# The Fourier step numbered by remainders to 64 and 47, with the first batch's blocks turned by TensorE

## The chip, the cores and the metric

The kernel runs on one core of one Trainium2 chip. A core has five engines with a queue of instructions each: TensorE (PE, with weight loads shown apart as PEld), VectorE (DVE), ScalarE (ACT), GpSimd (POOL) and SyncE (SP), which here only issues DMAs. An engine takes its instructions in the order of its queue; an instruction that waits for another engine holds up all that stands behind it.

The metric is the device time of one execution, as the median of several runs: 2486.35 us for the kernel before.

## What is computed

```python
X = np.fft.rfft(x, axis=1)                       # x: 8 batches, 3008 tokens, 256 columns
y = np.fft.irfft(X * (filt_r + 1j * filt_i), n=3008, axis=1)
h = y.reshape(24064, 256) @ w_in                 # 256 x 2048
g = h * (1.0 / (1.0 + np.exp(-1.702 * h)))
out = g @ w_out                                  # 2048 x 256
```

A real Fourier transform over 3008 tokens, a product with a filter, the transform back, and a two-layer network on every token. The weights come as 64-bit floats.

## The kernel before

**The transform.** 3008 = 64 x 47. Token 47 n1 + n2 stands at (n1, n2). The first step is, for each n2, a product with a 64 x 64 matrix over n1; in this numbering the matrix differs for every n2, since it holds the twiddle factors too. Pairs of n2 share the 128 rows: `t1` has 24 matrices, `t2` the 24 for the way back. The result is laid out by s (32 places), and the second step is, for each s, a product with a 47 x 47 matrix `d` over n2 (called s2 here). Then comes the product with the filter, then `e` (called i2), and last `t2` (i1). Between first and second step the data have to change places between partitions and columns. That goes through DRAM: `a_d` on the way in, `b_d` on the way back.

**Batch 0** is done by `first_fft` (from L301) before all else, in plain float32, in two halves of 128 columns. `load_t1` (L273) loads the first tables and spreads them with copies; `first_step` (L353) makes the first products (L360) and writes them to `a_d`; `load` reads them back into `z_zy` and `z_wi`; sixteen times follow s2 (L409), `product` (L429: three DVE instructions from PSUM, L433 to L435, and a sum on POOL, L436), i2 (L414), a copy on ACT (L415) and a store to `b_d` (L418). `load_f` loads a filter piece to partitions 0 to 47 and copies it to 64 to 111 on ACT (L333).

**Batches 1 to 7** are done by `fft` (L445) in pieces beside the network of the batch ahead, each operand split in a high and a low part in the float32r format (`mm3`, L257). L456 to L463 are its first step, `forward` and `backward` the others, with the same `product`, here from SBUF.

**The network.** 48 tiles of up to 512 tokens: `signal` (L552) makes i1 of the tile (L559) from `br` and splits it into `y`; `mlp` (L573) runs 16 chunks of h (L588, six products), the activation on ACT (L592, L593), the low part gl on DVE (L594) and six products into o (L602).

**The weights** are loaded and turned from 64-bit to two float32r parts by `weights` (L228) in 16 pieces, on ACT (L208, L218, L224), DVE (L213 to L219) and POOL (L217, L225). The first pieces are begun after `first_fft`, the others in the first tile's 16 chunks.

**What sets the order.** A scheduler orders each engine's queue by its own estimate of times; instructions given to `keep_in_program_order` stay as written. PSUM banks for batch 0 come in turn from three pools (`bank`, L265). SP's loads stay in program order until the middle of the first tile.

Of the kernel before, what the change touches and what calls it, by code (L numbers as in the profile page):

```python
# [17 lines left out]
N1, N2 = 64, 47  # L18
# [11 lines left out]
def _tables():  # L30
# [22 lines left out]
    t1 = np.zeros((P, NH, N1))  # L53
    t2 = np.zeros((P, NH, P))
    for j in range(2):
        for q in range(NH):
            n2 = NH + q if j else NH - 1 - q
            if n2 >= N2:
                continue
            for s in range(NS):  # L60
                if s == 0:
                    re, im = np.ones(N1), np.where(n1 % 2, -1.0, 1.0) * (-1.0 if j else 1.0)
                    ire, iim = re / S, im / S
                else:
# [34 lines left out]
    return t1.astype(np.float32), t2.astype(np.float32), de.astype(np.float32)  # L99


def _places():


    n1, q = np.arange(N1), np.arange(NH)
    n2 = np.stack([NH - 1 - q, NH + q])
    time = np.where(n2[:, None, :] < N2, N2 * n1[None, :, None] + n2[:, None, :], S)
    p, s = np.arange(48)[:, None], np.arange(NS)[None, :]
    high = np.where(s == 0, 32 + 64 * (p - 24), 64 - s + 64 * (p - 24))
    freq = np.where(p < 24, s + 64 * p, np.where((p < 47) | (s == 0), high, S // 2 + 1))  # L110
# [11 lines left out]
    return time, freq, np.concatenate(token)  # L122


def _layout(a):

    x, fr, fi, wi, wo = a
    time, freq, _ = _places()
    x = np.concatenate([x, np.zeros((B, 1, D), x.dtype)], 1)[:, time]
    x_0 = x[0].reshape(P, 3, 8, 2, P).transpose(3, 1, 0, 2, 4)  # L130
    x_r = x[1:].reshape(B - 1, P, 6, 4, D).transpose(0, 2, 1, 3, 4)
    f = np.stack([fr, fi], 1)
    f = np.concatenate([f, np.zeros((1, 2, D), f.dtype)])[freq]
# [7 lines left out]
def tile_kernel(  # L141
    ctx: ExitStack,
    tc: tile.TileContext,
    x_0: bass.AP,
    x: bass.AP,
    filt_0: bass.AP,
# [32 lines left out]
    t1_sb = const.tile([P, NH, 2, P], F32R, name="t1_sb")  # L179
    t2_sb = const.tile([P, NH, P], F32, name="t2_sb")  # L180
    de_sb = const.tile([Q, 2, 4, Q], F32R, name="de_sb")
    HALF = NFC // 2
    wi_sb, wo_sb = [], []
# [87 lines left out]
    t1_f, de_of = [], []  # L271

    def load_t1(q):  # L273
        hs = slice(12 * q, 12 * q + 12)
        st = sb.tile([P, 12, 2, 32], F32, tag="out", name=f"t1_{q}")
        load_in(st, t1[:, hs].rearrange("p h (k s) -> p h k s", k=2))
        tf = sb.tile([P, 12, 2, 2, 32], F32, tag="y", name=f"t1f_{q}")
        t1_f.append(tf.rearrange("p h j k s -> p h (j k s)"))
        nc.scalar.copy(tf[:, :, 0], st)
        for k in range(2):  # L280
            nc.vector.tensor_copy(tf[0:64, :, 1, k], st[0:64, :, 1 - k])
            nc.vector.tensor_scalar(tf[64:128, :, 1, k], st[64:128, :, 1 - k], -1.0, None, ALU.mult)

    def split_t1(q):
        hs = slice(12 * q, 12 * q + 12)
        nc.scalar.copy(t1_sb[:, hs, 0], t1_f[q])
        nc.vector.tensor_tensor(t1_sb[:, hs, 1], t1_f[q], t1_sb[:, hs, 0].bitcast(F32), ALU.subtract)

    def split_de(de_f):
# [3 lines left out]
        pin = tc.keep_in_program_order  # L293
        pin(nc.gpsimd.memset(de_sb.bitcast(F32), 0.0))
# [6 lines left out]
    def first_fft():  # L301
# [25 lines left out]
        def load_f(g, load_in=load_in):  # L327
# [4 lines left out]
            for i in range(0, n, 8):  # L332
# [3 lines left out]
                if i:  # L336
                    tc.keep_in_program_order(ins)
# [372 lines left out]
```

## Time and profile before

| what | value |
|---|---|
| device time, three runs | 2485.58, 2486.35, 2490.07 us |
| the profiled execution's own time | 2489.39 us |
| its span, first to last instruction | 2487.6 us |
| mean granted clock of TensorE | 0.987 |
| DMA traffic | 254.76 MB, 102 GB/s over the span |

The page of the profile gives busy time by engine; the groups of instructions give one row for each line, engine, operation and tile, with the mean of one; the waits say which engine stood idle until what. An engine's busy time says nothing of which stage it falls in, and a mean over the span mixes the opening with the long part behind it. The lines that matter stand in the prediction.

### The profile page before, as it was taken

How to read it: one execution, taken by the hardware profiler on the slowest of the kernel's cores; microseconds unless marked ns; L12 is line 12 of the kernel's file. 1: busy time of each engine (PE TensorE's matmuls, PEld its weight loads, DVE VectorE, ACT ScalarE, POOL GpSimd, SP SyncE). 2: the span in 40 equal slices, each digit the busy share in tenths (PEclk: the TensorE clock that was granted, in tenths of full speed). 3: DMA queues.
4: the chain of work that ended last, by engine and by line, in shares of the span. 5: the costliest groups of instructions: out<-in, count | busy, mean ns of one | idle time of the engine just before them, and what ended most of it. 6: DMA issues, size and time to landing. Idle time of an engine off the chain costs nothing.

```text
span 2487.6 us, 31904 instructions
## 1 busy us (share of the span) xinstructions
PE 2397.4 (96%) x11132; PEld 1986.7 (80%) x11132; DVE 1550.9 (62%) x2169; ACT 1315.1 (53%) x2399; POOL 825.9 (33%) x716
## 2 busy tenths in 40 slices
PE   5689999999999999999999999999999999999999
PEld 3368778878887888988888888888888888898887
DVE  6784895498636874478835787367753788432322
ACT  4555565555555555555555555555555555444443
POOL 3472553255324432254313443234421344100000
PEclk8789999999999999999999999999999999999999
DMA  8745443554345433544345343544434443300000
GB/s 202 213 123 148 103 114 103 150 109 113 98 136 118 107 85 90 153 99 106 75 135 126 94 96 83 148 113 104 101 92 129 101 105 83 73 15 9 18 9 18
DMA packets 154145, 254.76 MB, mean 102 GB/s; under 512 B 16112, under 2 KB 94048, under 8 KB 153696
## 3 DMA queue, kind: packets, MB, share of 16 engines
q1 hardware_dynamic: 71776, 137.46, 20.4%
q10 hardware_dynamic: 57056, 70.80, 10.8%
q0 software_dynamic: 25152, 44.45, 9.0%
q8 instruction: 89, 1.46, 0.2%
q14 instruction: 72, 0.59, 0.1%
HBM read 155.65 MB, written 96.99 MB: 102 GB/s over the span
## 4 chain that ended last, share of the span: by engine, by line
PE 75%; DMA 4%; DVE 2%; ACT 1%; issue 1%; SPq 0%; POOL 0%; ACTq 0%; POOLq 0%; DVEq 0%
PE o L602 33%; PE h L588 33%; PE i L559 3%; DMA br<-b_d 2%; PE s L494 2%; PE i L494 2%; DMA b_d<-b 1%; PE s L259 1%; PE s L260 1%; PE s L258 1%; DMA zy<-a_d 1%; DVE gl L594 1%; DMA a_d<-al 1%; DMA x<-in_x_dram 1%; SPq L174 0%
## 5 line engine op out<-in xcount | busy, mean ns | idle before, releaser
L588 PE MATMUL h<-y,wi 128*128 128x512 f32 (+1 forms) x4608 | 1174.6, 388 | 8.1 <-ACT wi L224 4.9
L594 DVE TENSOR_TENSOR gl<-g,gh 128x512 fp32r<-128x512 f32 (+1 forms) x768 | 648.3, 847 | 757.2 <-ACT gh L593 710.6
L588 PEld LDWEIGHTS h<-y,wi 128*128 128x128 f32 x4608 | 863.9, 189 | 178.9 <-ACT wi L224 5.4
L592 ACT ACTIVATE g<-h 128x512 f32<-128x512 f32 (+1 forms) x768 | 452.6, 590 | 926.3 <-PE h L588 820.8
L602 PE MATMUL o<-gh,wo 128*128 128x512 f32 (+1 forms) x3072 | 834.0, 390 | 8.4 <-ACT gh L593 6.4
L602 PEld LDWEIGHTS o<-gh,wo 128*128 128x128 f32 x3072 | 567.0, 189 | 122.7 <-ACT gh L593 11.1
L602 PE MATMUL o<-gl,wo 128*128 128x512 f32 (+1 forms) x1536 | 479.7, 388 | 9.4 <-DVE gl L594 9.3
L593 ACT ACTIVATE gh<-h 128x512 fp32r<-128x512 f32 (+1 forms) x768 | 449.0, 585 | 46.9 <-PE o L602 43.2
L509 POOL TENSOR_TENSOR zy<-c_buf,zy 48x512 fp32r<-48x512 f32 x224 | 330.9, 1477 | 92.1 <-DVE zy L508 82.0
L602 PEld LDWEIGHTS o<-gl,wo 128*128 128x128 f32 x1536 | 285.2, 189 | 67.1 <-DVE gl L594 13.6
L436 POOL TENSOR_TENSOR c_buf<-c_buf,u_buf 112x512 f32<-112x512 f32 x128 | 183.3, 1432 | 465.7 <-DVE c_buf L435 464.6
L456 POOL TENSOR_TENSOR xl<-x,xh 128x512 fp32r<-128x512 f32 x84 | 112.6, 1352 | 416.1 <-ACT xh L455 357.5
L477 POOL DMA_DIRECT2D zy<-a_d x224 | 128.1, 574 | 293.6 <-DMA a_d<-ah 80.1
L443 DVE TENSOR_TENSOR c_buf<-s,c_buf 48x512 f32<-48x512 f32 x224 | 154.1, 688 | 22.5 <-ACT c_buf L442 16.4
L443 DVE TENSOR_TENSOR b<-i,b 48x512 f32<-48x512 f32 x224 | 154.0, 687 | 8.4 <-ACT b L442 2.0
L442 ACT COPY c_buf<-s 48x512 f32<-48x512 f32 x224 | 130.2, 581 | 19.9 <-PE s L494 9.8
L442 ACT COPY b<-i 48x512 f32<-48x512 f32 x224 | 130.1, 581 | 14.5 <-PE i L494 4.1
L559 PEld LDWEIGHTS i<-t_sb,br 128*128 128x128 f32 x736 | 101.5, 196 | 36.4 <-DVE w_tu L215 8.2
L508 DVE CAST zy<-c_buf 48x512 fp32r<-48x512 f32 x224 | 100.0, 447 | 44.4 <-POOL c_buf L436 40.5
L559 PE MATMUL i<-t_sb,br 128*128 128x128 f32 x736 | 106.4, 282 | 21.9 <-DMA br<-b_d 20.9
L570 POOL CAST y<-carry 128x128 fp32r<-128x128 f32 x8 | 3.2, 429 | 266.0 <-PE h L588 265.9
L434 DVE TENSOR_TENSOR u_buf<-c_buf,f_buf 48x512 f32<-48x512 f32 x112 | 87.1, 778 | 3.6
(91 smaller groups left out, 1343.9 us busy)
## 6 DMA issues: line engine op xcount, KB each, us to landing
f_buf<-in_filt_dram SPq DMA_DIRECT2D x224, 192.0 KB, 3.3
zy<-a_d POOLq DMA_DIRECT2D x224, 192.0 KB, 3.6
x<-in_x_dram SPq DMA_DIRECT2D x48, 512.0 KB, 4.9
b_d<-b ACTq DMA_DIRECT2D x128, 192.0 KB, 2.6
out_dram<-out SPq DMA_DIRECT2D x44, 512.0 KB, 3.7
a_d<-ah ACTq DMA_DIRECT2D x84, 256.0 KB, 3.5
a_d<-al ACTq DMA_DIRECT2D x84, 256.0 KB, 3.8
br<-b_d SPq DMA_DIRECT2D x84, 256.0 KB, 4.7
```

The costliest lines, as they stand in the source:

```text
L436: nc.gpsimd.tensor_tensor(u1, u1, u2, ALU.add)
L442: nc.scalar.copy(dst[h], ps[k][o])
L443: nc.vector.tensor_tensor(dst[h], ps[k][h], dst[h], ALU.add)
L456: nc.gpsimd.tensor_tensor(xl, src, xh.bitcast(F32), ALU.subtract)
L477: nc.gpsimd.dma_start(zy[0][64 * k : 64 * k + 48, i % 2].rearrange("p k s d -> p k (s d)"), src.rearrange("n k s d -> n k (s d)"),)
L509: nc.gpsimd.tensor_tensor(y[o, k], u1[h], y[h, k].bitcast(F32), ALU.subtract)
L559: nc.tensor.matmul(ps[:, P * i : P * i + P], br[m][:, i], t2_sb[:, 4 * t + i, :], start=True, stop=True)
L588: nc.tensor.matmul(ps[:, :w], wi_sb[half][:, wk, kc, c], y[:, yk, kc, :w], start=n == 0, stop=n == 5)
L592: nc.scalar.activation(g[:, :w], ps[:, :w], AF.Gelu_apprx_sigmoid)
L593: nc.scalar.activation(gh[:, :w], ps[:, :w], AF.Gelu_apprx_sigmoid)
L594: nc.vector.tensor_tensor(gl[:, :w], g[:, :w], gh[:, :w].bitcast(F32), ALU.subtract)
L602: nc.tensor.matmul(pos[m][:, :w], wo[:, wk, P * m : P * m + P], gp[gk][:, :w], start=fc == 0 and n == 0, stop=fc == NFC - 1 and n == 2,)
```

## The change

**Numbering.** Place (n1, n2) now holds token (47 n1 + 64 n2) mod 3008, and a frequency is numbered by its remainders to 64 and to 47. In this numbering the two steps separate: the first matrix is the same for all n2, so `t1` and `t2` are one 128 x 128 matrix each. In exchange some of the needed frequencies stand where their mirror image is computed, so the imaginary part of the product needs a sign by place: `sign`, one column per s. `product` takes two s with different signs at a time, and reads the sign per partition: four DVE instructions of 256 columns in place of two of 512.

**Tables.** All tables come in one DRAM tensor `tabs` and lie in one SBUF tile `tab`; the first 128 columns are loaded by a DMA of their own.

**Batch 0 stays on chip.** The first step takes x as the stationary operand, so its result has columns of x on the partitions; ACT and DVE copy it to `a_t` ordered by s. For each pair of s TensorE transposes four blocks of `a_t` into PSUM, ACT copies them to `zs`, and s2 follows. i2 takes the product as the stationary operand, in four products of 96 columns, and ACT copies the result to `b_t`. `signal` transposes blocks of `b_t` into PSUM, and ACT or DVE copies them to `br`. `a_d` and `b_d` of batch 0, and the ACT copies of the filter, are gone; each filter piece is now loaded by two DMAs.

**Batches 1 to 7** keep their way through DRAM. `mm3` in the first step now covers two n2 in one go of 512 columns.

```diff
-                for i in range(2):
-                    h = 4 * c + 2 * u + i
-                    mm3(ps[:, i, :], t1_sb[:, h, 0, :], t1_sb[:, h, 1, :], xh[:, i, :], xl[:, i, :])
+                mm3(ps, t1_sb[:, 0], t1_sb[:, 1], xh, xl)
...
-        nc.vector.scalar_tensor_tensor(u2[0:48], xs[64:Q], -1.0, f_i[64:Q], ALU.mult, ALU.mult)
-        nc.vector.tensor_tensor(u2[64:Q], xs[0:48], f_i[0:48], ALU.mult)
+        for u in range(2):
+            for h, o in ((slice(0, 48), slice(64, Q)), (slice(64, Q), slice(0, 48))):
+                sg = sign[h, 2 * i + u : 2 * i + u + 1]
+                nc.vector.scalar_tensor_tensor(u2[o, u], xs[h, u], sg, f_i[h, u], ALU.mult, ALU.mult)
         nc.vector.tensor_tensor(u1, xs[:Q], f_r, ALU.mult)
         nc.gpsimd.tensor_tensor(u1, u1, u2, ALU.add)
...
+        w = WIDTHS["t1_0"]
+        pin(nc.scalar.dma_start(tab[:, 0:w], tabs[:, 0:w]))
+        xrs = [raw(f"x_0_{c}") for c in range(6)]
+        for c in range(6):
+            load_in(xrs[c], x[0, c])
+            if c == 3:
+                pin(nc.scalar.dma_start(tab[:, w:], tabs[:, w:]))
...
+        for c in range(6):
+            for m in range(2):
+                ps = bank(f"s1_0_{c}_{m}").rearrange("p a d -> p (a d)").rearrange("p (i c) -> p i c", i=4)
+                for i in range(4):
+                    nc.tensor.matmul(ps[:, i], xrs[c][:, i, P * m : P * m + P], table["t1_0"], start=True, stop=True)
+                src = ps.rearrange("p i (a s) -> p s a i", s=NS)
+                dst = a_t[m].rearrange("p s (a q) -> p s a q", q=NH)[:, :, :, 4 * c : 4 * c + 4]
+                (nc.vector.tensor_copy if m else nc.scalar.copy)(dst, src)
+        yield
+        for g in range(16):
+            if 6 <= g + 6 < 16:
+                load_f(g + 6)
+            z_ps = bank(f"z_0_{g}")
             for u in range(2):
+                for m in range(2):
+                    nc.tensor.transpose(z_ps[:96, u, P * m : P * m + P], a_t[m][:, 2 * g + u], table["eye"])
+            z = sb.tile([96, 2, D], F32, tag="half", name=f"zs_0_{g}", bufs=4)
+            nc.scalar.copy(z, z_ps[:96])
+            ps = bank(f"s2_0_{g}")
+            ms = [(slice(0, 1), 1), (slice(1, 2), 0)] if g == 0 else [(slice(0, 2), 0)]
+            for u, m in ms:
+                nc.tensor.matmul(ps[:Q, u], d_0[:96, m], z[:, u], start=True, stop=True)
+            u1 = c_buf[g % 3]
+            product(g, ps, u1, f_s[g % 8])
+            ps = bank(f"i2_0_{g}").rearrange("p a d -> p (a d)")[:, 0:384].rearrange("p (m u c) -> p m u c", m=2, u=2)
+            for u in range(2):
+                for m in range(2):
+                    nc.tensor.matmul(ps[:, m, u], u1[:Q, u, P * m : P * m + P], e_0[:Q, int(g + u == 0)], start=True, stop=True)
+            nc.scalar.copy(b_t[:, :, :, 2 * g : 2 * g + 2], ps.rearrange("p m u c -> p m c u"))
             yield
...
+            if b == 0:
+                ps = ps_f.tile([P, 4, P], F32, tag="f", name=f"bt_{t}_{m}")
+                for i in range(4):
+                    q = 4 * (4 * t + i)
+                    nc.tensor.transpose(ps[:, i], b_t[:, m, q : q + 4].rearrange("p c s -> p (c s)"), table["eye"])
+                br = {m: sb.tile([P, 4, P], F32, tag="half", name=f"br_{b}_{t}_{m}", bufs=4)}
+                (nc.vector.tensor_copy if m else nc.scalar.copy)(br[m], ps)
...
-        if i in (4, 5, 6):
+        if i in (2, 5, 8, 11):
             run(w_parts, 1)
-        if i == 5:
-            br = next(first_b)
-    next(first_b)
-    run(w_parts, 5)
-    run(start(0, 0, br))
+    run(w_parts, 4)
+    run(start(0, 0))
```

TensorE's queue in `first_fft`, from the first i2 on, before. The name `s_0_5` is s2 of group 5, `i_0_1` is i2 of group 1 (L409 and L414):

```order
L409 MATMUL s_0_2_264<-z_zy,de_f 112x512
L409 MATMUL s_0_3_273<-z_zy,de_f 112x512
L409 MATMUL s_0_4_287<-z_zy,de_f 112x512
L414 MATMUL i_0_0_246<-c_buf_78,de_f 112x128
L414 MATMUL i_0_0_246<-c_buf_78,de_f 112x384
L409 MATMUL s_0_5_296<-z_zy,de_f 112x512
L414 MATMUL i_0_1_256<-c_buf_79,de_f 112x512
L409 MATMUL s_0_6_315<-z_zy,de_f 112x512
L414 MATMUL i_0_2_270<-c_buf_80,de_f 112x512
```

The same place now; `z_2` names the four transpositions (L342) of group 2, copied to `zs_2` on ACT before s2 of group 2 can read it:

```order
L348 MATMUL s_0_0_208<-zs_0_206,tab 112x256 x2
L354 MATMUL i_0_0_217<-tab,c_buf_78 128x96 x4
L348 MATMUL s_0_1_232<-zs_1_230,tab 112x512
L342 MATMUL z_2_250<-tab,a_t_85 96x128
L342 MATMUL z_2_250<-tab,a_t_86 96x128
L342 MATMUL z_2_250<-tab,a_t_85 96x128
L342 MATMUL z_2_250<-tab,a_t_86 96x128
L348 MATMUL s_0_2_257<-zs_2_255,tab 112x512
L354 MATMUL i_0_1_240<-tab,c_buf_79 128x96 x4
```

Before, s2 of groups 0 to 4 stood ahead of i2 of group 0, and s2 stayed five ahead. Now s2 of group 1 stands behind i2 of group 0, and s2 of group 2 ahead of i2 of group 1. The queue goes on in the same way in turn, to the end of the sixteen groups:

```order
L354 MATMUL i_0_2_265<-tab,c_buf_80 128x96 x4
L348 MATMUL s_0_3_280<-zs_3_278,tab 112x512
L342 MATMUL z_4_296<-tab,a_t_85 96x128
L342 MATMUL z_4_296<-tab,a_t_86 96x128
L342 MATMUL z_4_296<-tab,a_t_85 96x128
L342 MATMUL z_4_296<-tab,a_t_86 96x128
L348 MATMUL s_0_4_303<-zs_4_301,tab 112x512
L354 MATMUL i_0_3_288<-tab,c_buf_78 128x96 x4
```

So the s2 of every odd group moved behind the i2 of the even group ahead of it.

DVE's queue in the middle of the program, where batch 3's transform runs beside the network: one group before (`c_buf` holds s2's result, `gl_1_10` is the low part of chunk 10 of a tile):

```order
L443 TENSOR_TENSOR c_buf_78<-s_3_6_1_7323,c_buf_78 48x512
L434 TENSOR_TENSOR u_buf_81<-c_buf_78,f_buf 48x512
L433 SCALAR_TENSOR_TENSOR u_buf_81<-c_buf_78,f_buf 48x512
L594 TENSOR_TENSOR gl_1_10_6752<-g_1_10_6750,gh_1_10_6751 128x512
L435 TENSOR_TENSOR c_buf_78<-c_buf_78,f_buf 112x512
```

and the same group now:

```order
L374 TENSOR_TENSOR c_buf_78<-s_3_6_1_7467,c_buf_78 48x512
L365 SCALAR_TENSOR_TENSOR u_buf_81<-c_buf_78,tab,f_buf 48x256 x4
L521 TENSOR_TENSOR gl_1_12_6953<-g_1_12_6951,gh_1_12_6952 128x512
L366 TENSOR_TENSOR c_buf_78<-c_buf_78,f_buf 112x512
```

Four instructions of half the width stand ahead of gl where two stood.

More of the change, by code (lines that the diff above doesn't have):

```diff
@@ L149, in tile_kernel @@
     w_out: bass.AP,
-    t1: bass.AP,
-    t2: bass.AP,
-    de: bass.AP,
+    tabs: bass.AP,
     out: bass.AP,
@@ L176, in load_in @@
             tc.keep_in_program_order(ins)
-    t1_sb = const.tile([P, NH, 2, P], F32R, name="t1_sb")
-    t2_sb = const.tile([P, NH, P], F32, name="t2_sb")
+    tab = const.tile([P, sum(WIDTHS.values())], F32, name="tab")
+    t1_sb = const.tile([P, 2, P], F32R, name="t1_sb")
     de_sb = const.tile([Q, 2, 4, Q], F32R, name="de_sb")
     HALF = NFC // 2
+    table, at = {}, 0
+    for name, w in WIDTHS.items():
+        table[name] = tab[:, at : at + w]
+        at += w
+    t2_sb, sign = table["t2"], table["sign"]
     wi_sb, wo_sb = [], []
@@ L269, in bank, with split_de @@
         return pool.tile([P, 2, D], F32, tag=tag, name=name)
[L271 to L289, printed above, removed]
+    def split_de():
         pin = tc.keep_in_program_order
+        de_f = table["de"].rearrange("p (m c) -> p m c", m=4)
+        pin(nc.scalar.copy(t1_sb[:, 0], table["t1"]))
+        pin(nc.vector.tensor_tensor(t1_sb[:, 1], table["t1"], t1_sb[:, 0].bitcast(F32), ALU.subtract))
         pin(nc.gpsimd.memset(de_sb.bitcast(F32), 0.0))
@@ L314, in first_fft @@
-        f_in = [f_0, f_1[0], f_1[1], f_2[0], f_2[1], f_1[0], f_1[1], f_0]
-        f_loads = {0: (1, f_0), 1: (2, f_1[2]), 3: (1, f_2[0]), 4: (1, f_2[1]), 5: (2, f_1[2]), 7: (1, f_0)}
-        def clean(eng, *ts):
-            for t in ts:
-                tc.keep_in_program_order(eng.memset(t[32:64], 0.0))
-        clean(nc.vector, f_0)
-        clean(nc.gpsimd, *c_buf)
-        a_d = [dram1.tile([48, 64, H], F32, name=f"a_d0_{i}") for i in range(2)]
-        b_d = b_of[0] = [dram1.tile([48, 64, H], F32, name=f"b_d0_{i}") for i in range(2)]
@@ new lines, in first_fft @@
+        d_0 = table["d_0"].rearrange("p (m c) -> p m c", m=2)
+        e_0 = table["e_0"].rearrange("p (m c) -> p m c", m=2)
+        a_t = [const.tile([P, NS, 96], F32, tag=t, name=f"a_t{m}") for m, t in enumerate(("wi_1", "wo_1"))]
+        f_s = [f_buf] + [sb.tile([Q, 4, 2, D], F32, tag="y", name=f"f_y{i}") for i in range(2)]
+        f_s = [f[:, 2 * i : 2 * i + 2] for f in f_s for i in range(2)]
+        f_s += [sb.tile([Q, 2, 2, D], F32, tag="out", name=f"f_o{i}") for i in range(2)]
+        pin = tc.keep_in_program_order
@@ new lines, in first_fft @@
+        for g in range(8):
+            pin((nc.gpsimd if g < 6 else nc.vector).memset(f_s[g][32:64], 0.0))
+        for g in range(6):
+            load_f(g)
+        for c in range(6):
[6 more added lines that the diff above has]
+                (nc.vector.tensor_copy if m else nc.scalar.copy)(dst, src)
```

244 lines of the change are left out of this document (70 added, 174 removed).

## The prediction

> **What bounds the kernel now.** I read the page first, then busy time by stage, then who waits for whom, then the order of time in the opening.
>
> ```profile
> span 2487.6 us, 31904 instructions
> PE 2397.4 (96%) x11132; PEld 1986.7 (80%) x11132; DVE 1550.9 (62%) x2169; ACT 1315.1 (53%) x2399; POOL 825.9 (33%) x716
> ```
>
> 96% for PE is a mean over unlike stages. By stage (columns: length, busy time of PE, PEld, DVE, ACT, POOL, then granted clock, DMA share, GB/s):
>
> ```profile
> 0.00:100.00 100.00, 57.73 (x187) 34.68 (x188) 66.98 (x83) 42.38 (x46) 36.08 (x32) 0.83 0.82 212
> 100.00:150.00 50.00, 37.93 (x137) 28.09 (x135) 46.54 (x65) 29.94 (x53) 33.58 (x20) 0.86 0.50 151
> 150.00:200.00 50.00, 43.68 (x195) 35.14 (x196) 34.34 (x39) 29.14 (x55) 30.69 (x21) 0.93 0.46 126
> 200.00:2000.00 1800.00, 1776.96 (x8401) 1485.09 (x8400) 1194.22 (x1684) 990.52 (x1829) 667.88 (x594) 1.00 0.45 111
> ```
>
> From 200 us on PE is busy 98.7% of the time, so there only PE work added or removed counts. Before that there are two other bounds. From 100 to 150 us DVE is busy 46.54 of 50: it prepares the weights of the first tile. From 0 to 100 us no engine is full. PE's waits, first up to 200 us, then after it:
>
> ```profile
> PE i L559 <- DMA br<-b_d: 14.5, 3, 7.4
> PE s L360 <- DVE t1f L282: 13.3, 1, 13.3
> PE s L360 <- DMA x<-in_x_dram: 9.8, 3, 5.1
> ...
> PE o L602 <- DVE gl L594: 6.4, 5, 1.8
> ```
>
> So the change aims at real waits: 13.3 us for the tables, 14.5 us for batch 0 on its way back from DRAM. But what the first tile needs is the weights, and DVE does those after the last product of batch 0. The points in order of time that matter (PE, DVE, POOL and ACT):
>
> ```profile
> 13.32 8.04 PE L360 MATMUL s<-x,t1f 128*128 128x128 f32 x48 [13.32 <-DVE t1f L282]
> 45.86 1.12 PE L414 MATMUL i<-c_buf,de_f 112*112 112x128 f32 x4
> 61.64 1.02 PE L409 MATMUL s<-z_wi,de_f 112*112 112x512 f32 x2
> 98.90 5.29 PE L588 MATMUL h<-y,wi 128*128 128x512 f32 x12 [1.43 <-ACT wi L224]
> ...
> 42.25 0.69 DVE L433 SCALAR_TENSOR_TENSOR u_buf<-s,f_buf 48x512 f32<-48x512 f32 x1 [1.12 <-PE s L409]
> 42.98 0.68 DVE L434 TENSOR_TENSOR u_buf<-s,f_buf 48x512 f32<-48x512 f32 x1
> 43.69 0.69 DVE L435 TENSOR_TENSOR c_buf<-s,f_buf 112x512 f32<-112x512 f32 x1
> 81.66 0.69 DVE L435 TENSOR_TENSOR c_buf<-s,f_buf 112x512 f32<-112x512 f32 x1
> 90.22 0.43 DVE L213 TENSOR_SCALAR w_tu<-w_tu 128x512 f32<-128x512 f32 x1 [4.77 <-ACT w_tu L208]
> 44.54 1.27 POOL L436 TENSOR_TENSOR c_buf<-c_buf,u_buf 112x512 f32<-112x512 f32 x1 [32.64 <-DVE c_buf L435]
> 46.61 1.27 POOL L436 TENSOR_TENSOR c_buf<-c_buf,u_buf 112x512 f32<-112x512 f32 x1 [0.80 <-DVE c_buf L435]
> 88.08 0.58 ACT L415 COPY b<-i 112x512 f32<-112x512 f32 x1 [0.15 <-PE i L414]
> ```
>
> The 16 products run from 42.25 to 82.35, one every 2.16 us but for one stall. The weights begin on DVE at 90.22, and the first h at 98.90. Everything up to about 180 us hangs on that 90.22, since DVE is then the bound. **The question is when DVE starts on the weights after the change.**
>
> **The start gets earlier.** The first table was in use at 3.95:
>
> ```profile
> 3.95 8.17 DVE L281 COPY t1f<-t 64x384 f32<-64x384 f32 x1 [0.94 <-DMA t<-in_t_dram]
> ...
> 5.00:10.00 5.00, 0.00 (x0) 0.00 (x0) 5.00 (x1) 0.00 (x0) 5.00 (x4) 1.00 1.03 317
> ```
>
> That was 384 KB issued at 0.76; x_0 (512 KB) now goes first with a 64 KB table, so PE starts at about 4.5 us instead of 13.3. The six pieces of x and the rest of the table are 3.8 MB, 12 us at 317 GB/s, so x ends near 15. PE needs 8.04 us for the first 24 small fp32 products (the x48 row, two records each) and, at the warm price of 0.2 us each below, 4.8 for the other 24: the step ends at about 17.3. A copy (0.69), four transpositions (up to 0.8), a copy (0.58) and s2 (1.02) later, with 0.6 for hand-overs, the first product begins at 21.0, against 42.25. I bound this by 19 and 25.
>
> **The products get slower, and this takes the lead back.** In before PE's queue holds s2 of four or five groups ahead of the first i2, so DVE never waits for POOL. Now (the rows are in the part on the change) i2 of g stands ahead of s2 of g+1 for every even g: i2_0, s2_1, then z_2, s2_2, i2_1, then z_3, i2_2, s2_3. PE works in order, and i2 waits for POOL's sum. So for every second product DVE waits until its own previous result has been through POOL and i2. Price of the loop from one POOL sum to the second next: POOL to PE 0.05 (the sum of 44.54 ends at 45.81, i2 starts at 45.86); four i2; s2 1.02; to DVE 0.1 (an estimate, between the two hand-overs beside it); two products; to POOL 0.14 (43.69 + 0.69 to 44.54 is 0.16); POOL 1.27.
> - i2: four products of 96 columns. The nearest rows are the small fp32 products at full clock, eight records (four products) in the 0.80 us until the next row starts, 0.2 each, so 0.8:
>
> ```profile
> 183.61 1.05 PE L559 MATMUL i<-t_sb,br 128*128 128x128 f32 x8
> 184.41 1.62 PE L588 MATMUL h<-y,wi 128*128 128x512 f32 x6
> ```
>
> - A product is now five DVE instructions, four of 48x256 with a sign read per partition, one of 112x512. No row shows 256 columns; two widths of one kind bound it:
>
> ```profile
> L568 DVE TENSOR_TENSOR y<-i,y 128x512 fp32r<-128x512 f32 x80 | 52.2, 684 | 5.1 <-ACT y L567 4.6
> L568 DVE TENSOR_TENSOR y<-i,y 128x64 fp32r<-128x64 f32 x8 | 1.7, 217 | 0.0
> ```
>
> 1.04 ns per column, so 256 take 0.42 us, between 0.217 and 0.684. With 0.03 between instructions (42.25 + 0.69 to 42.98 is 0.04, 42.98 + 0.68 to 43.69 is 0.03) a product costs 4 x 0.45 + 0.72 = 2.5, where 2.16 was.
> The loop: 0.05 + 0.8 + 1.02 + 0.1 + 5.0 + 0.14 + 1.27 = 8.4 us for two products, where 4.3 was. PE idles some 40% of it, so I take its clock as in the mixed stage from 100 to 150 us, 0.86: (0.8 + 1.02)/0.86 adds 0.3, **8.7**. The seven loops cost 61 us. From 21.0: first product and sum 3.9, seven loops 60.9, then i2, s2 and the last product 4.8: the products end at 90.6 (82.35 before). POOL 1.4, i2 0.85, copy 0.58 and the first step on ACT 0.7 follow: **DVE turns to the weights at about 94 us, 4 later than before**. The 20 us won at the front are given back. The wait that went (br from DRAM) is replaced by PE's wait for POOL.
> What follows is as long as before: the order gives DVE the same 16 weights and their rows; a br copy more (0.69) stands against a memset less (1.8). The DMAs taken away (a_d, b_d, late pieces of t2) and the 12 us of ACT copies of the filter were off this chain after 90 us. Filters come as eight pieces ahead, 3.1 MB behind x, 10 us at 317 GB/s: landed by 26, while the sixth product begins beyond 40. On SP's queue the first four weights stand among reloads of filters that wait for products up to the eighth: issued by about 60, well before 94.
>
> **After 200 us.** (a) Of 48 transpositions of b_t, those of tiles 2 to 5, 32 in all, fall where PE is full. No row shows one; between 0 and the 0.2 of the fp32 row I take 0.2, **+6.4**. (b) The first step of batches 1 to 7 is three products of 512 columns per PSUM bank for six of 256:
>
> ```profile
> 153.75 0.28 PE L258 MATMUL s<-xh,t_sb 128*128 128x256 f32 x1
> 153.98 0.28 PE L260 MATMUL s<-xh,t_sb 128*128 128x256 f32 x1
> 177.11 2.89 PE L588 MATMUL h<-y,wi 128*128 128x512 f32 x12
> 179.84 0.62 PE L602 MATMUL o<-gh,wo 128*128 128x512 f32 x2
> ```
>
> From start to start 0.115 each for 256, (179.84 - 177.11)/12 = 0.2275 for 512: 84 x (0.690 - 0.683) = 0.6; the last of a group hides some, I take **-1** (bounds 0 and -2). (c) In batches 1 to 7 the product's two instructions become four:
>
> ```profile
> L434 DVE TENSOR_TENSOR u_buf<-c_buf,f_buf 48x512 f32<-48x512 f32 x112 | 87.1, 778 | 3.6
> L433 DVE SCALAR_TENSOR_TENSOR u_buf<-c_buf,f_buf 48x512 f32<-48x512 f32 x112 | 78.2, 699 | 3.6
> ```
>
> 112 x (4 x 0.45 - 1.48) = 36 us more for a DVE that has 606 of 1800 idle. Behind these four stands gl, for which PE waits 6.4 us today. Bounds 0 and 36; DVE is mostly idle, so I take **+2**.
> Sum: 4 + 6.4 - 1 + 2 = +11. The profiled execution took 2489.39 us (span 2487.6 and 1.8 around it), 3.0 above the median of 2486.35; with 11 more it would be 2500.4, and the median 2497.
>
> A rule against the row of (a): the Trainium skill, "TensorE: Matmul & The Clock Gate", section "Terms", says transposition mode is four times faster for fp32. By it the 32 would cost 1.6 (an estimate), and the sum would be 2492. No run here shows a transposition yet.
>
> **Rivals.**
> 1. *The loop does not bite* (faster). If s2 could run ahead as it does now, 16 products at 2.5 take 40 us, end at 61, and the weights start at 64.7: 25.5 us earlier, with +7.4 behind, 2468. For it: the trace keeps 2.16 us at L435 to L436 as long as s2 is ahead. Against it: the order's rows leave no room on an in-order queue. Chance 0.08; it decides if the products' starts are even.
> 2. *Nothing measurable.* Clock full (8.4, products end 2.1 earlier), transpositions near nothing, DVE hidden: +2 + 1.5 - 1, about 2489. Chance 0.2.
> 3. *The clock falls.* PE's clock is lower after idle stretches:
>
> ```profile
> 45.00:50.00 5.00, 3.81 (x10) 1.11 (x8) 4.80 (x8) 3.44 (x3) 3.31 (x3) 1.00 1.14 342
> 65.00:70.00 5.00, 4.03 (x8) 2.07 (x9) 0.59 (x1) 2.59 (x2) 0.20 (x1) 0.66 1.01 202
> 80.00:85.00 5.00, 2.94 (x10) 2.42 (x11) 2.49 (x5) 0.58 (x1) 2.52 (x2) 0.50 0.73 221
> ```
>
> At half clock i2 and s2 take 3.6 instead of 1.8, and the second s2 of a loop, behind four transpositions at 0.4, a copy and itself at 2.04, comes 1.7 after DVE is free: 8.4 + 1.8 + 1.7 = 11.9, 3.2 more than 8.7, times seven 22, and 3 at both ends: 2522. Against it: the waits in the loop are about 2 us, shorter than the 3.69 before the row of 80 to 85. Chance 0.12. The Trainium skill says it stronger, in the same page, "Part 4: PE-mode transpose": transpositions do not count as activity for the clock. No row of before can show that.
> 4. *DVE is not hidden.* A good half of the 36 us comes through in the steady part as waits for gl: +20, 2515. Speaks for it that POOL and DVE already slow each other (L434 778 against L433 699 ns). Chance 0.1.
>
> **How the numbers follow.** My forecast, its own range 2491.5 to 2508, has 0.5. Faster by over 0.2% (about 5 us, what a measurement here can tell from no change): rival 1 and a little, 0.1. Within 0.2%: 0.2. Slower: 0.7. The range 2479 to 2521 leaves out rival 1 and the worst half of rival 3.
>
> **What would show it.** The new products (DVE, 112x512 into c_buf) start in pairs, 2.5 and 6 us apart in turn; PE's wait at i2 is on POOL; the first starts near 21, the last ends near 91; DVE's first weight row near 94, first h near 102. Even starts prove rival 1. A clock under 0.7 from 25 to 90 us is rival 3. After 200 us, PE's idle time before gl products well over 6.4 us is rival 4. I am wrong if the weights start before 85 us or if PE's added work after 200 us is not some 5 us.

## The result and the profile after

The changed kernel takes 2530.68 us (median of 4 runs, 2529.24 to 2532.68), the kernel before 2486.31: a ratio of 1.0176, interval 1.0158 to 1.0194. It is slower, as forecast, but by 44 us instead of 11, beyond the range's upper end of 2521. The page, and busy time by stage (columns as before):

```profile
span 2529.2 us, 31965 instructions
PE 2441.0 (97%) x11082; PEld 2005.1 (79%) x11082; DVE 1601.1 (63%) x2423; ACT 1301.9 (51%) x2409; POOL 831.3 (33%) x714
...
0.00:100.00 100.00, 76.29 (x290) 52.38 (x290) 41.82 (x77) 19.15 (x34) 22.00 (x23) 0.64 0.49 141
100.00:150.00 50.00, 36.78 (x136) 27.17 (x137) 37.60 (x60) 22.66 (x40) 22.87 (x15) 0.63 0.18 53
150.00:200.00 50.00, 34.01 (x119) 23.57 (x118) 49.44 (x55) 27.77 (x53) 34.80 (x23) 0.86 0.25 74
200.00:2000.00 1800.00, 1770.03 (x8133) 1463.72 (x8132) 1230.56 (x1861) 985.67 (x1824) 673.98 (x588) 1.00 0.44 111
```

In the first 100 us PE is busy for 76.29 us, where it was 57.73, at a granted clock of 0.64, where it was 0.83. It does more there than before (290 records for 187), and does it more slowly. The points in order of time (PE, then DVE; first product, one pair of products, last product, weights):

```profile
19.79 0.60 PE L342 MATMUL z<-tab,a_t 128*96 128x128 f32 x4
20.73 1.12 PE L348 MATMUL s<-zs,tab 96*112 96x256 f32 x4 [0.34 <-ACT zs L344]
26.16 2.02 PE L354 MATMUL i<-tab,c_buf 112*128 112x96 f32 x8 [4.31 <-POOL c_buf L367]
27.97 1.94 PE L348 MATMUL s<-zs,tab 96*112 96x512 f32 x2
29.70 1.06 PE L342 MATMUL z<-tab,a_t 128*96 128x128 f32 x4
31.44 2.05 PE L348 MATMUL s<-zs,tab 96*112 96x512 f32 x2 [0.67 <-ACT zs L344]
34.15 2.02 PE L354 MATMUL i<-tab,c_buf 112*128 112x96 f32 x8 [0.66 <-POOL c_buf L367]
...
21.94 2.03 DVE L365 SCALAR_TENSOR_TENSOR u_buf<-s,tab,f_buf 48x256 f32<-48x256 f32 x4 [2.47 <-DMA f_y<-in_filt_dram]
24.00 0.69 DVE L366 TENSOR_TENSOR c_buf<-s,f_buf 112x512 f32<-112x512 f32 x1
32.06 0.69 DVE L366 TENSOR_TENSOR c_buf<-s,f_buf 112x512 f32<-112x512 f32 x1
35.64 0.69 DVE L366 TENSOR_TENSOR c_buf<-s,f_y 112x512 f32<-112x512 f32 x1
104.79 0.69 DVE L366 TENSOR_TENSOR c_buf<-s,f_o 112x512 f32<-112x512 f32 x1
112.78 0.69 DVE L366 TENSOR_TENSOR c_buf<-s,f_o 112x512 f32<-112x512 f32 x1
118.07 0.43 DVE L224 TENSOR_SCALAR w_tu<-w_tu 128x512 f32<-128x512 f32 x1 [4.60 <-ACT w_tu L219]
```

The products do start in pairs (8.06 and 3.58 apart), and PE's wait at i2 is on POOL. From the first pair to the eighth, 24.00 to 104.79, seven loops take 80.8 us, 11.5 each. An s2 takes 2.05 and four of the 96-column products 2.02, twice what they take below at full clock: PE runs at half clock for nearly all of 25 to 113 us (only from 88.9 to 92.3 is it full). The stretch where the clock was lost (same columns):

```profile
23.00:24.00 1.00, 0.00 (x0) 0.00 (x0) 0.94 (x2) 0.00 (x0) 0.00 (x0) 1.00 1.04 254
24.00:25.00 1.00, 0.00 (x0) 0.00 (x0) 0.69 (x1) 0.00 (x0) 0.16 (x1) 0.52 1.07 242
...
25.00:113.00 88.00, 69.42 (x206) 42.86 (x206) 38.86 (x75) 15.42 (x29) 18.77 (x15) 0.52 0.29 80
```

PE had nothing to do from 21.85 us (20.73 + 1.12) until POOL's first sum at 26.16; some 2 us into that wait the clock fell, and over the 88 us of the loop it is 0.52 on average although PE is busy for 69 of them.

The end of the first tile is the first copy of `out`. Before and after (duration least, median, most, then the first and the last start):

```profile
L615 DVE COPY out<-o x48: 558/692/694, 182.4 to 2482.4; 128x512 f32<-128x512 f32 x44, 128x384 f32<-128x384 f32 x4
```
```profile
L542 DVE COPY out<-o x48: 556/691/695, 211.2 to 2524.4; 128x512 f32<-128x512 f32 x44, 128x384 f32<-128x384 f32 x4
```

The profiled execution before took 3.1 us more than the median, the one after 0.3 more. So the 41.6 us between the two spans, where the medians are 44.4 apart, fall into three parts: the weights begin 27.9 us later (118.07 against 90.22); the first tile takes 0.9 more from there (93.1 against 92.2); the rest, from the end of the first tile to the end of the span, takes 12.8 more (2318.0 against 2305.2). The forecast had 4, 0 and 7.4.

### The profile page after: what moved, and what is told of

Read it like the earlier page. It is cut to its first block, busy times and chain, and to the rows that moved or that the text cites. A ratio compares the mean times of both kernels' runs of the same rounds, so it can differ in the third digit from the quotient of the medians.

```text
span 2529.2 us, 31965 instructions
## 1 busy us (share of the span) xinstructions
PE 2441.0 (97%) x11082; PEld 2005.1 (79%) x11082; DVE 1601.1 (63%) x2423; ACT 1301.9 (51%) x2409; POOL 831.3 (33%) x714
## 4 chain that ended last, share of the span: by engine, by line
PE 73%; DMA 4%; DVE 3%; issue 1%; ACT 1%; SPq 0%; POOL 0%; ACTq 0%; POOLq 0%; DVEq 0%
PE o L529 32%; PE h L515 32%; PE i L486 3%; DMA br<-b_d 2%; PE s L423 2%; PE i L423 1%; DVE u_buf L365 1%; PE s L270 1%; PE s L269 1%; PE s L271 1%; DVE c_buf L374 1%; DVE gl L521 1%; DMA x<-in_x_dram 1%; DMA b_d<-b 1%; DMA zy<-a_d 1%
## 5 line engine op out<-in xcount | busy, mean ns | idle before, releaser
L367 POOL TENSOR_TENSOR c_buf<-c_buf,u_buf 112x512 f32<-112x512 f32 x128 | 192.4, 1503 | 517.5 <-DVE c_buf L366 517.2
L365 DVE SCALAR_TENSOR_TENSOR u_buf<-c_buf,tab,f_buf 48x256 f32<-48x256 f32 x448 | 225.4, 542 | 6.6
L486 PEld LDWEIGHTS i<-tab,br 128*128 128x128 f32 x736 | 100.5, 195 | 26.8 <-issue 9.4
L486 PE MATMUL i<-tab,br 128*128 128x128 f32 x736 | 104.7, 280 | 13.6 <-DMA br<-b_d 9.6
```

The costliest lines, as they stand in the source:

```text
L365: nc.vector.scalar_tensor_tensor(u2[o, u], xs[h, u], sg, f_i[h, u], ALU.mult, ALU.mult)
L367: nc.gpsimd.tensor_tensor(u1, u1, u2, ALU.add)
L486: nc.tensor.matmul(ps[:, P * i : P * i + P], br[m][:, i], t2_sb, start=True, stop=True)
```

## The experiments

Two questions: why the clock stays at half in the loop, and what the 12.8 us of the rest are made of. Times are medians, where there was more than one run; ratios are to the kernel before on the same chip, whose median was 2490.5, 2489.6 and 2490.4 us in the three sessions.

| kernel | clock, stretch (us) | weights begin | first tile ends | rest | time | ratio (interval) |
|---|---|---|---|---|---|---|
| before | 0.83, 0 to 100 | 90.2 | 182.4 | 2305.2 | 2486.3 | 1 |
| changed | 0.52, 25 to 113 | 118.1 | 211.2 | 2318.0 | 2530.7 | 1.0176 (1.0158 to 1.0194) |
| e11_after (changed, again) | 0.56, 25 to 111 | 116.1 | 209.2 | 2321.3 | 2533.0 | 1.0170 (1.0156 to 1.0184) |
| e1_ahead | 0.89, 25 to 70 | 70.1 | 161.3 | 2325.4 | 2485.9 | 0.9985 (0.9976 to 0.9994) |
| e2_plain | 0.76, 25 to 104 | 108.4 | 200.3 | 2320.8 | 2523.4 | one run |
| e3_twice | 0.67, 25 to 109 | 113.7 | 205.7 | 2319.4 | 2527.9 | one run |
| e5_bridge | 0.50, 35 to 112 | 116.3 | 209.5 | 2326.4 | 2537.6 | one run |
| e6_filled | 1.00, 25 to 95 | 99.7 | 192.5 | 2323.3 | 2517.6 | one run |
| e12_fill_t | 1.00, 25 to 95 | 97.4 | 192.5 | 2321.0 | 2515.4 | one run |
| e4_two | 0.52, 25 to 113 | 118.0 | 211.1 | 2311.8 | 2521.4 | 1.0121 (1.0104 to 1.0137) |
| e9_before4 | 0.93, 50 to 75 | 90.0 | 184.1 | 2311.1 | 2495.8 | 1.0017 (1.0008 to 1.0025) |
| e10_halves | 0.52, 25 to 113 | 117.7 | 210.6 | 2324.3 | 2534.6 | 1.0174 (1.0160 to 1.0188) |
| e7_turned | 0.88, 25 to 70 | 69.6 | 161.5 | 2317.6 | 2483.6 | 0.9977 (0.9968 to 0.9985) |
| e8_early | 0.88, 25 to 70 | 62.3 | 160.3 | 2319.1 | 2482.0 | 0.9973 (0.9962 to 0.9985) |

The column "rest" is of one execution each. The changed kernel itself gave 2318.0 and 2321.3, and with e1, e2, e3, e5, e6 and e12, which have the same instructions behind the first tile, the range is 2318.0 to 2326.4. So differences of up to 8 us in it mean little by themselves.

**e1_ahead: the same instructions, another order on PE.** In the loop, all pinned on PE:

```diff
+        turn(0)
+        for g in range(2):
+            turn(g + 1)
+            step2(g)
         for g in range(16):
...
-            z_ps = bank(f"z_0_{g}")
...
-            product(g, ps, u1, f_s[g % 8])
+            product(g, ss.pop(g), u1, f_s[g % 8])
+            turn(g + 3)
+            step2(g + 2)
             ps = bank(f"i2_0_{g}")...
```

`turn` is the four transpositions and the copy to zs, `step2` is s2.

> PE's order in batch 0 is written out: the transpositions of group g+3 and s2 of group g+2 stand ahead of i2 of group g, so PE no longer waits for a POOL sum or for a zs copy before it can go on. Same instructions, other order. Theory GAPS (the granted clock stays at 0.50 from 25 to 113 us because waits of 0.7 us break every stretch of PE's work): with the waits gone the clock goes to 1.00 for most of 25 to 70 us, the products start every 2.8 us (DVE's own 2.03 + 0.69 + gaps), the last one ends near 68 us instead of 113.5, DVE's weights begin near 72 instead of 118, and the time is about 2530.7 - 46 = 2485 us. Theory KIND (the clock stays low because of what PE runs there: transpositions, and products of 96 columns that are mostly weight loads): the clock stays at 0.50 although PE is busy without a break, a product every 5.0 us (2.02 + 1.94 + 1.06), the last ends near 100, the weights begin near 105, time about 2518 us.

Measured: the weights begin at 70.13 us, the time is 2485.9. PE in its loop, then busy time and clock of five us there (columns as before):

```profile
39.30 1.13 PE L370 MATMUL i<-tab,c_buf 112*128 112x96 f32 x8 [0.36 <-POOL c_buf L383]
40.27 0.60 PE L344 MATMUL z<-tab,a_t 128*96 128x128 f32 x4
40.71 1.02 PE L354 MATMUL s<-zs,tab 96*112 96x512 f32 x2
42.08 1.13 PE L370 MATMUL i<-tab,c_buf 112*128 112x96 f32 x8 [0.35 <-POOL c_buf L383]
```
```profile
35.00:40.00 5.00, 4.29 (x25) 2.61 (x24) 4.68 (x11) 2.04 (x4) 2.53 (x2) 1.00 0.73 170
```

One product every 2.78 us (39.30 to 42.08), paced by DVE, which is busy 4.68 of 5. The clock is 1.00 with the same transpositions and 96-column products in the queue. It fell here too, at 26.0 us, after a first wait of 1.71 us, and came back at 29.4, after 3.4 us in which PE did not wait. GAPS predicted 2485, KIND 2518. These rows also give prices at full clock: four products of 96 columns 0.97 (39.30 to 40.27), four transpositions 0.44, so **0.11 each**.

**e2_plain and e3_twice: more work for PE in the same loop.** In e2 the four transpositions are ordinary fp32 products, in e3 each is done twice:

```diff
-                    nc.tensor.transpose(z_ps[...], a_t[m][:, 2 * g + u], table["eye"])
+                    nc.tensor.matmul(z_ps[...], a_t[m][:, 2 * g + u], table["eye"], start=True, stop=True)   (e2)
+                    for _ in range(2):                                                                     (e3)
+                        nc.tensor.transpose(z_ps[...], a_t[m][:, 2 * g + u], table["eye"])
```

> The 64 transpositions of a_t are ordinary fp32 products with the unit matrix; nothing else changes. At half clock four of them should take about 2.05 us instead of 1.06 (the fp32 product of the same size in i1, eight records in 2.05). Theory GAPS: the waits of 0.7 us stay, the clock stays near 0.50, two products take 11.65 + 2 x 1.0 = 13.6 us, time about 2530.7 + 8 x 2 = 2546 us. Theory KIND with the transpositions as the cause: the clock rises to 0.85 or more from 25 us on, two products take about 9 us, the last product ends near 95, time about 2512 us.

> Each of the 64 transpositions of a_t is done twice into the same place, so PE is as long at it as e2_plain is (about 2.1 us for a group at half clock), but in transposition mode. Both theories expect a granted clock of 0.50 and about 2546 us. Together with e2_plain: if e2_plain's clock rises and this one's does not, the mode is the cause; if both stay low, the gaps are; if both rise, the length of the unbroken stretch is.

Both expectations missed: neither kernel got slower, and both clocks rose (0.76 and 0.67 where it was 0.52). By the rule in the expectation, both rising means that it is the length of the unbroken stretch. Each is one run, and e11_after, the changed kernel itself, came to 0.56, so e3's rise is small against that. e3 adds 64 transpositions that do nothing and brings the weights forward by 4.4 us (by 2.4 against the second execution of the changed kernel, e11_after): at half clock the longer stretch of i2, s2 and transpositions wins the clock back more often (eight times in e2's loop and five in e3's, against once in the changed kernel and three times in e11_after), and it is lost again in the waits.

**e5_bridge and e6_filled: the waits filled.** PE's order as in the changed kernel, written out; `idle(n)` puts n small products ahead, whose results are overwritten or not read. e5 fills only the first wait, e6 all of them:

```diff
+        def idle(ps, n):
+            for _ in range(n):
+                pin(nc.tensor.matmul(ps[:, 0:P], table["t1_0"], table["eye"], start=True, stop=True))
...
+            idle(ps[:, 384:512], n)      ahead of i2: 20 for the first; e6 also 8 and 6 in turn
+            idle(ss[g]..., n)            ahead of s2: e6 3 for every second group
```

> PE's order of the changed kernel, written out word for word, with one addition: 20 small fp32 products (128 columns, results not used) stand ahead of the first i2, where PE waited 4.31 us for the first POOL sum. Theory ONE STALL (the clock falls in that one wait, and a loop that runs at half clock cannot win it back): with the wait filled the clock stays near 1.00 in the loop, two products take 8.4 + 2 x 0.28 = 9.0 us instead of 11.65, the weights begin near 97 instead of 118, time about 2510 us. Theory LOOP (the loop itself loses the clock, since at full clock PE has work for only some 60% of it, in stretches of 2 us): the first two or three products run at full clock, then the clock is 0.50 again and the loop 11.65; weights near 113, time 2525 to 2530 us.

> As e5_bridge, and every wait in the loop is filled as well: 3 small products ahead of s2 (wait for the zs copy), 8 and 6 ahead of the two i2 (wait for POOL). It adds PE work of some 3.4 us at full clock to each two products and takes away no instruction. If gaps alone hold the clock down: 1.00 from 27 us to the last product, two products in 9.0 to 9.5 us, the last one ends near 95, weights near 100, time about 2512 us, some 18 faster than the changed kernel for more work. If it is the kind of work that holds it down (transpositions and products of 96 columns are still there): the clock stays 0.50, the fillers cost 0.5 us each, two products take about 17 us, time about 2570 us.

e5: the first loop ran at full clock, then it was gone. Its PE rows and the clock there:

```profile
29.26 1.11 PE L355 MATMUL s<-zs,tab 96*112 96x512 f32 x2 [0.67 <-ACT zs L348]
32.39 2.02 PE L369 MATMUL i<-tab,c_buf 112*128 112x96 f32 x8 [2.02 <-POOL c_buf L399]
```
```profile
30.00:31.00 1.00, 0.37 (x1) 0.00 (x0) 0.96 (x2) 0.00 (x0) 0.00 (x0) 1.00 0.46 94
31.00:32.00 1.00, 0.00 (x0) 0.00 (x0) 0.94 (x2) 0.00 (x0) 0.93 (x1) 0.67 0.15 37
```

The clock fell 1 us after PE's last work, in a wait of 2.02 us; from 35 to 112 us the clock is 0.50. Theory LOOP holds, ONE STALL falls. (The time of 2537.6 is higher than LOOP expected, from a rest of 2326.4 in this execution.) e6:

```profile
25.00:95.00 70.00, 66.67 (x474) 55.58 (x472) 39.24 (x75) 15.45 (x29) 19.00 (x15) 1.00 0.39 106
```

With 66.67 of 70 us busy the clock is 1.00, and from 24.20 to 88.16 seven loops take 64.0, **9.1 us each**. More work, and 13.4 us off the span (2515.8 against 2529.2). e6 differs from the changed kernel by its fillers and by the written-out order, which e5 has too at a clock of 0.50, so **the low clock is worth 2.4 us in each loop**.

**e12_fill_t: transpositions as fillers.** e6 with `nc.tensor.transpose` in `idle` and twice the numbers (40, 6, 16, 12).

> As e6_filled, but the fillers are transpositions, twice as many of half the length (40 ahead of the first i2, then 6, 16 and 12), so PE is as busy as in e6_filled, more than half of it with transpositions. If a transposition counts for the clock like a product: 1.00 from 27 us to the last product, two products in 9.1 us, weights near 100 us, time as e6_filled's, about 2517 us. If transpositions do not count: the clock falls to 0.50 within 30 us as in e5_bridge, the 34 fillers of two products cost 0.26 each, two products take 16 to 18 us, and the time is 2565 us or more.

```profile
25.00:95.00 70.00, 64.76 (x460) 52.02 (x460) 39.36 (x75) 15.45 (x29) 19.02 (x15) 1.00 0.39 107
...
49.31 1.13 PE L369 MATMUL i<-tab,c_buf 112*128 112x96 f32 x8 [0.29 <-POOL c_buf L399]
50.28 0.60 PE L346 MATMUL z<-tab,a_t 128*96 128x128 f32 x4
50.72 1.47 PE L340 MATMUL i<-tab 128*128 128x128 f32 x12
```

Of the 9.1 us of a loop more than half are transpositions, and the clock is 1.00. So these transpositions count for the clock.

**e4_two and e9_before4: the product's four instructions in the rest.** e4 takes them out of batches 1 to 7 of the changed kernel (the sign by place is left out there), e9 puts four, with the signs as constants, into batches 1 to 7 of the kernel before:

```diff
+        if xs is u1:
+            a, o = slice(0, 48), slice(64, Q)                                                         (e4)
+            nc.vector.scalar_tensor_tensor(u2[o], xs[a], -1.0, f_i[a], ALU.mult, ALU.mult)
+            nc.vector.tensor_tensor(u2[a], xs[o], f_i[o], ALU.mult)
...
+        for u in range(2) if xs is u1 else ():                                                        (e9)
+            for h, o, sg in ((slice(0, 48), slice(64, Q), 1.0), (slice(64, Q), slice(0, 48), -1.0)):
+                nc.vector.scalar_tensor_tensor(u2[o, u], xs[h, u], sg, f_i[h, u], ALU.mult, ALU.mult)
```

> In batches 1 to 7 the product's imaginary part is two DVE instructions of 512 columns again, as in the kernel before, so the sign by place is left out there; batch 0 keeps the four. DVE has 112 x (4 x 0.5 - 1.48), about 58 us, less to do. If the four instructions are what lengthens the part behind the first tile (from the end of the first tile at 211.2 us to the end of the span it is 2318.0 us, where it was 2305.2), that part falls by 5 us to about 2313 and the time to about 2526 us. If DVE's work is hidden there, it stays within 1 us of 2318.0 and the time within 1 us of 2530.7. The opening stays as it is (clock 0.50, weights near 118 us).

> The kernel before, in which only the product of batches 1 to 7 is made of four DVE instructions of 256 columns, with the signs as constants. It is the third of the changed kernel's terms behind the first tile by itself. If DVE's extra work (112 x (4 x 0.45 - 1.48) = 36 us or more) comes through as it did between the changed kernel and e4_two (6.2 us in the part behind the first tile): about 2486.3 + 6 = 2492.5 us, ratio 1.0025. If it is hidden, as the prediction took it (+2): ratio 1.001 or less. If it comes through by half: 2505, ratio 1.0075.

The rest fell by 6.2 us in e4 (2311.8), and grew by 5.9 in e9 (2311.1); e9's time grew by a ratio of 1.0017, 2 to 6 us by its interval. e4's time fell by more than expected: its ratio is 1.0121 against 1.0170 and 1.0176 for the changed kernel in two other sessions, which is 12 to 14 us (7 to 18 by the intervals against e11_after). Its profiled execution was the slowest of its four, so its rest may say too little; why the time fell by more than 6 us is not known. The groups of the four, in the changed kernel, and in e9 where the sign is a constant:

```profile
L365 DVE SCALAR_TENSOR_TENSOR u_buf<-c_buf,tab,f_buf 48x256 f32<-48x256 f32 x448 | 225.4, 542 | 6.6
```
```profile
L435 DVE SCALAR_TENSOR_TENSOR u_buf<-c_buf,f_buf 48x256 f32<-48x256 f32 x448 | 194.1, 472 | 5.9
```

Read with the 165.3 us of the two instructions before (87.1 + 78.2), DVE has 60 us more to do in the changed kernel, of which 6 (by the rest) to 14 (by the times) reach the end, and 29 us more in e9, of which 4 to 6 do.

**e10_halves: the merged mm3 split again.**

```diff
-                mm3(ps, t1_sb[:, 0], t1_sb[:, 1], xh, xl)
+                for i in range(2):
+                    mm3(ps[:, i], t1_sb[:, 0], t1_sb[:, 1], xh[:, i], xl[:, i])
```

> The changed kernel with mm3 in batches 1 to 7 split again into two times three products of 256 columns. The prediction's term for the merge was -1 (bounds 0 and -2): the time rises by 1 us against e11_after, ratio 1.0005 apart. A rival: six products of 256 columns cost PE 0.28 each in a row (the mean that the groups show), the merge had saved 84 x (6 x 0.28 - 3 x 0.40) = 40 us, and the time rises by 40.

> The changed kernel as it is, for comparison on the same chip: ratio to before within 0.002 of 1.0176.

Apart by a ratio of 0.0004 (1.0174 against 1.0170), 1 us, less than either interval: by these the merge can be worth some 6 us at most, and not the 40 that the means of the groups suggest.

**e7_turned and e8_early: the transpositions moved, and a version that beats both.** e7 is e1_ahead with the transpositions of tiles 1 to 5 during the first tile:

```diff
+    def turn_b(t, m):
+        q = 16 * t
+        ps = ps_f.tile([P, 4, P], F32, tag="f", name=f"bt_{t}_{m}")
+        for i in range(4):
+            nc.tensor.transpose(ps[:, i], b_t[:, m, q + 4 * i : q + 4 * i + 4]..., table["eye"])
+        nc.scalar.copy(b_t[:, m, q : q + 16]..., ps...)
...
                 run(w_parts, 1)
+                if 1 <= fc <= 10:
+                    turn_b((fc + 1) // 2, (fc + 1) % 2)
```

> e1_ahead, and the transpositions of b_t for tiles 1 to 5 are all made during the first tile, where PE idles a third of the time, each copied by ACT back into its own place in b_t; i1 reads it there. If the 32 transpositions of tiles 2 to 5 cost PE 0.27 us each behind the first tile (PE's work there is 8.7 us more than in the kernel before), the part behind the first tile falls from 2325.4 by 8.7 to about 2317, the first tile stays within 3 us of its 80 us, and the time is about 2478 us, ratio to before 0.996. If they cost nearly nothing there (a quarter of an fp32 product's 0.2, 1.6 us in all), the time is within 2 us of e1_ahead's 2485.9, ratio 0.998.

> e7_turned, and the first four steps of the weights on ACT are issued three products earlier, ahead of the last copies of batch 0, so that DVE goes from its last product straight to the weights instead of waiting 4.6 us. If DVE's start on the weights sets the end of the first tile: DVE's first rows for the weights come near 66 instead of 70, the first tile ends 4 us earlier, time about 2474 us. If something else sets it (the copies of b_t and i1 for the first tile, the fetch of the weights), less than 1 us.

e7 gained 2 us on e1 (0.9977 against 0.9985, with intervals that overlap), not 8; its rest fell by 7.8, but e1's own 2325.4 stands high among the executions, so the medians decide: near the lower of the two expectations. What the 32 cost where PE is full, the changed kernel's own trace shows; one of their eight groups of four and the row behind it:

```profile
333.96 0.60 PE L481 MATMUL bt<-tab,b_t 128*128 128x128 f32 x4
334.31 1.18 PE L529 MATMUL o<-gh,wo 128*128 128x512 f32 x4
```

From start to start that is 0.35 for four, so 2.8 us for the 32. e8 issues the weights' first steps on ACT three products earlier (one more `yield` in `weights`, one more step of it at group 13). DVE's first row for the weights came at 62.3, yet the first tile ended only 1.2 us earlier and the time moved by 1.6, inside the intervals: something else sets the first h, which came at 79.8 against 82.3. What it is was not followed up. At 2482.0 us, ratio 0.9973, e8 beats the kernel before by 0.15 to 0.38% and the changed kernel by some 50 us.

## Why the prediction was wrong

**What was right.** The order of PE's queue, read before the run, did what the text said: products in pairs, PE waiting for POOL at i2, DVE held up behind it. The first product came at 21.94 (21.0, bounds 19 to 25). The first tile took as long as before from the weights on (0.9 us more). The sign of the result, and that the lead from the earlier start is given back, follow from this: with a full clock (e6) the kernel was still slower than before.

**The step that failed** is the clock in the loop: "PE idles some 40% of it, so I take its clock as in the mixed stage from 100 to 150 us, 0.86". It was 0.52. Rival 3 had the case and nearly the number, 11.9 us a loop (measured 11.5), but a chance of 0.12, because "the waits in the loop are about 2 us, shorter than the 3.69 before the row of 80 to 85". That sentence took the length of one wait for the rule, and it does not decide: in e5 the clock went in a wait of 2.02 us. The trace of the kernel before had shown it already, since PE's wait ahead of the row of 65 to 70, at a clock of 0.66, was 2.45 us. The wait that comes before the loop was not looked at either: PE has no work from its s2 of 20.73 to POOL's first sum, 4.31 us, so the loop already starts at half clock. That matters little, as e5 fills this wait and still loses the clock within one loop.

What decides can be read from all fourteen traces. Between 20 and 200 us (300 in the kernel before and the changed one) the clock changes 180 times, and in each trace all changes lie a whole number of steps of 3.41 us apart, to within 0.01 us. At the end of such a step the clock fell only where the profile has PE busy for 0.64 of the step or less (below 0.47 it always fell), and it came back only after a step with 0.83 or more, though some full steps did not bring it back. Two steps of the kernel before, at whose ends the clock fell, and two of the changed kernel, after the first of which it stayed at half and after the second of which it came back:

```profile
49.18:52.59 3.41, 1.30 (x3) 0.63 (x4) 3.25 (x6) 0.00 (x0) 2.11 (x2) 1.00 0.95 221
62.83:66.24 3.41, 0.96 (x3) 0.27 (x2) 1.00 (x2) 0.00 (x0) 1.47 (x2) 1.00 1.01 323
...
58.17:61.58 3.41, 2.66 (x13) 2.21 (x13) 1.41 (x3) 1.06 (x2) 1.26 (x1) 0.50 0.86 233
85.47:88.88 3.41, 3.41 (x11) 1.98 (x10) 0.52 (x2) 0.48 (x1) 0.00 (x0) 0.50 0.00 0
```

At full clock PE has work for about half of a loop (4.9 of 9.1 us by the prices of e1, an estimate), so the clock is soon lost. At half clock the waits shrink to 0.7 us and PE is busy for 0.79 of the loop, but its stretches without a wait are 4.6 us at most, so few of the steps fall wholly into one. How often one does depends on where the steps begin, which differs from one execution to the other; two of the same kernel had 0.52 and 0.56. The kind of work seems to count too: in the loops of the changed kernel, e2 to e5, e10 and e11, ten full steps with an s2 and at most 1.31 us of i2 brought the clock back, and ten with an s2 and 1.41 us or more of i2 did not. No run tests that by itself. A mean over a stage with long fp32 runs in it was no stand-in for a loop of short ones.

**The term mis-sized by it.** Seven loops were priced at 61 us and took 80.8. Of the 20 us, 2.4 in each loop, 17 in all, are the clock (11.5 against e6's 9.1 with full clock). The other 3 are prices: a product of five DVE instructions 2.78 instead of 2.5, four 96-column products 0.97 instead of 0.8 at full clock, less the 0.3 that the text had added for a clock of 0.86. The first product and the ends add 4, and the weights begin at 118.1 instead of 94. These 24, 0.9 in the first tile and 5.4 behind it are 30 of the 33.7 us between the forecast of 2497 and the 2530.7; the 3.1 by which the profiled execution before lay above its median are most of the rest.

**After the first tile** 7.4 us were forecast and 12.8 measured (16.1 in e11_after). (a) The 32 transpositions were taken at 0.2 each; they took 0.09, so 2.8 instead of 6.4. The Trainium skill, "TensorE: Matmul & The Clock Gate", section "Terms", would have had 1.6 (an estimate): the ratio there is four, measured here 0.2 to 0.09, about two. (b) The merge: -1 was not contradicted. (c) The four DVE instructions: +2 was forecast; e9 shows 4 to 6 (with constant signs) and e4 6 to 14, within the bounds 0 and 36. The +20 of rival 4 is above both; its place is not refuted. PE's waits from 200 us on in the changed kernel, then its wait for gl in e4_two and in e9_before4 behind the first tile (us in all, times, longest):

```profile
PE i L486 <- DMA br<-b_d: 9.6, 12, 2.1
PE o L529 <- ACT gh L520: 7.4, 9, 1.9
PE s L420 <- DMA zy<-a_d: 5.6, 4, 3.4
PE o L529 <- DVE gl L521: 4.4, 7, 1.2
```
```profile
PE o L534 <- DVE gl L526: 1.6, 3, 0.8
```
```profile
PE o L606 <- DVE gl L598: 9.1, 8, 2.3
```

For gl PE waits 4.4 us, less than the 6.4 of the kernel before, so the sign by which the text wanted to know rival 4 did not come. But with the two instructions it is 1.6 (e4), and with four in the kernel before it is 9.1 instead of 6.4: 2.8 and 2.7 us may be waits for gl. But the changed kernel's second execution waited 6.0 us for gl, so differences of this size are hardly clear of the spread. Where the rest of the cost lies no row shows. Of the 12.8, 2.8 + 6 - 1 leave 5 us that no run accounts for; with the 12 us of e4's times for the four instructions nothing would be left. Which of the two holds stays open.

**Rivals.** 1 (the loop does not bite) is what e1_ahead makes true by order: its products start evenly. It gets 2485.9, not 2468, because the weights begin at 70.1 and not at 64.7, and because its rest is 20 us longer than before (one execution) and not 7.4. 3 came true in the opening. By the Trainium skill, same page, "Part 4: PE-mode transpose", the transpositions would have been the reason; e12 contradicts it for these fp32 transpositions, with a clock of 1.00 while they fill more than half of PE's time.

## What to carry to other kernels

Where PE waits in a loop at all, price the loop at half clock and at full clock, take PE's busy share in each, and ask which of the two states keeps itself up; here a loop that started at full clock (e5) fell back at once. The cure is the order: put the next groups' independent work ahead of the instruction that waits, on the in-order queue. A rising busy share of PE at a falling granted clock is lost time, not use.

## What the runs showed of the hardware that was not expected

- In the stretches looked at, the clock changed only on a grid of 3.41 us, by how busy PE had been in the step that ended there (the figures stand in the part above). So the fall came between 1.0 us (e5) and 4.5 us (e3_twice, 21.27 to 25.79 us) after PE's last work, and waits of 1.65 us (changed kernel, 90.89 to 92.54) and 1.71 us (e1_ahead) were enough. The Trainium skill, "TensorE: Matmul & The Clock Gate", "Part 1: The HAM clock gate (the "warmup" mystery)", speaks of an idle window of about 3.4 us; the length agrees with the grid here, but the window need not be idle throughout: in e5 PE was busy for 1.78 us of it.
- Work that does nothing can make a kernel faster: e6_filled and e12_fill_t have 13.4 and 15.7 us less span than the changed kernel (2515.8 and 2513.5 against 2529.2).
- An instruction of 48x256 with a sign read per partition took DVE 542 ns in the rest of the changed kernel, one with a constant 472 ns in e9. The sign need not be the whole reason: the 112x512 instruction behind them took 714 against 686 ns in the same two kernels.
- At full clock a 128x128 fp32 transposition follows the last after 0.09 us (the rows of 333.96) to 0.11 us (e1), and a product of 96 columns takes 0.24.
